# New ranks for GpSimd's free work in a top-k attention and channel-mix kernel

## The chip, the cores and the metric

The kernel runs on one core of one Trainium2 chip. The metric is the device time of one execution in microseconds. It has four engines that compute here: TensorE (PE in the profile, with PEld for its weight loads), VectorE (DVE), ScalarE (ACT) and GpSimd (POOL); SyncE (SP) issues the transfers.

## The reference

Two layers, one after the other, in float32. Attention with 8 batches, 8 heads, 576 positions and 64 numbers per head keeps, for each query, only the keys whose score reaches the 32nd largest; the channel mix shifts each sequence by one position, mixes it with itself in two ways and puts it through three matrices.

```python
scores = scale * np.matmul(q, k.transpose(0, 1, 3, 2))
kth = np.partition(scores, -32, axis=-1)[..., -32:-31]
scores = np.where(scores >= kth, scores, -1000000000.0)
attn = np.exp(scores - scores.max(-1, keepdims=True))
x = np.matmul(attn / (attn.sum(-1, keepdims=True) + 1e-09), v)   # then (8, 576, 512)
x_prev = np.concatenate([np.zeros((B, 1, D)), x[:, :-1, :]], axis=1)
xk = mu_k * x + (1.0 - mu_k) * x_prev
xr = mu_r * x + (1.0 - mu_r) * x_prev
k = np.maximum(xk @ w_k, 0.0)            # 512 -> 1024
v = k * k @ w_v                          # 1024 -> 512
r = 1.0 / (1.0 + np.exp(-(xr @ w_r)))
return r * v
```

## The kernel before

**Attention.** The 4608 rows of all batches are cut into 18 blocks of 256; a block has four groups (a pair of heads each), a group has four tiles of 128 rows by 576 keys, 288 tiles in all. A tile goes through a pipeline of some eight steps: scores on PE (`ps`), a copy by ScalarE (`sc`), the largest eight of each of seven pieces and three rounds over these on DVE (`cand`, `seen`), a signed copy on ScalarE and a product on GpSimd (`sg`, line 263) for the last eight of the 32, the exponentials (`se`), the masked product `E` on DVE, transposes on PE (`pt`) and their copy (`et`). At the end of a group come the inverses of the row sums: ScalarE adds the 1e-9 and DVE takes the reciprocal (`rs`, line 294), GpSimd spreads it (`rb`, line 298), PE transposes it (line 305), and after the value matmuls of the group (line 318) ScalarE copies the sums and GpSimd writes the product into `xT` (line 326).

**The mix.** A block is also a chunk (0 to 17) of the channel mix, which works in float32 split into a rounded part and a remainder, with three matmuls per product (`three`). A chunk has two halves of the 512 channels; a half is there when two of the four groups are placed in `xT`. `begin` queues the difference (`xd`), the share (`xm`) and the sum (`xm`) for a half, `finish` the rounded input (`xh`, ScalarE) and its remainder (`xl`, GpSimd). That is done twice for a chunk, first for the gates (`which` is 1), then for the hidden layer. `gates` is 8 pieces of PE work (`pz`), `hiddens` 16 pieces in four blocks of 256 hidden channels (`ph`); each block is followed by a relu and a rounded square on ScalarE (`r`, `hh`) and, on GpSimd, by the square (`r`, line 390) and its remainder (`hl`, line 391). `values` is twice 8 pieces (`pv`), one for each half of the rows: the first half is issued while the next chunk's gate inputs are made ready, the second after that chunk's gates, while its hidden inputs are made ready. If the next chunk isn't complete when the hidden blocks end, both halves are issued at once. The first value pieces use the first hidden blocks, the seventh the last.

**The order.** Everything is issued in an order that the program writes out itself. In one turn of its loop, here called slot n, every stage takes one step: scores of tile n, transposes of tile n - 5, and so on through the list ORDER; `mix` then issues pieces of the channel mix. Slot n's scores are the n-th group of line 213 or 217 in the trace. Free work waits in a queue for each lane (ScalarE, GpSimd) and has a price, a list of what it must follow, and a rank; a ledger says how much is issued in a slot:

```python
PACE, TENSOR, SHARE, PIECE, CAP, MOST = 4.60, 3.45, 0.74, 0.72, 4.45, 4
END, HASTE = 36, 0.56
...
while (item := self.first(self.queue.get(place, []))) and self.free[place] >= item.cost * SHARE * ...:
    self.do(item)
...
able = [item for item in queue if all(a.done for a in item.after)]
return min(able, key=lambda item: item.rank, default=None)
```

At the end of a slot a lane gets 4.60 us (never more than 4.45 in all), PE 3.45 (3.75). The fixed work is taken off as it is issued: on GpSimd 1.36 in each slot for `sg`, 0.34 in a slot with n divisible by 4 (`rb`), 0.6 two slots later (the product into `xT`); on ScalarE 2.56 in each slot, 0.25 in the slot after `rb`, 0.4 in the one after that, 0.46 for a relu, 0.48 for a gate's tanh. On PE 1.15 goes for scores and transposes, 1.54 more in the slot after `rb`, and 0.72 for a piece, from slot 252 on 0.56; no more than four pieces are issued in a slot. A piece that depends on free work (`past`) is issued only in a slot after the one in which that work was issued. Of items with equal rank the one queued first is taken.

Ranks before: `begin` 0, `finish` 0 (2 after slot 291, when DVE takes over GpSimd's free work), hidden blocks 1.

Of the kernel before, what the change touches and what calls it, by code (L numbers as in the profile page):

```python
# [9 lines left out]
F32 = mybir.dt.float32  # L10
# [3 lines left out]
AF = mybir.ActivationFunctionType  # L14
# [32 lines left out]
def topk_attention_channel_mix(ctx: ExitStack, tc: tile.TileContext, q, k, v, mu_k, mu_r, w_k, w_v, w_r, out):  # L47
    nc = tc.nc
# [279 lines left out]
    def begin(g, C, which, i, L):  # L328

        X, h0, n, pieces = Env(), 2 * i, C.n, C.pieces  # L330
        C.begun += 1
        parts, o = [], 0
        for xT, s, m in pieces:
            parts.append((o, xT, s, m))
            o += m

        def change():
            g.change[i] = g.one.tile([128, 2, CH], F32, name=f"xd{h0}")
            for o, xT, s, m in parts:
                g.by.tensor_sub(g.change[i][:, :, o:o + m], xT[:, h0:h0 + 2, s:s + m], xT[:, h0:h0 + 2, s + 1:s + 1 + m])  # L340

        def share():
            X.xm = g.two.tile([128, 2, CH], F32, name="xm")
            for h in (0, 1):
                g.by.tensor_scalar(X.xm[:, h, :n], g.change[i][:, h, :n], nmu[:, which, h0 + h:h0 + h + 1], 1.0, op0=OP.mult, op1=OP.mult)

        def add():
            for o, xT, s, m in parts:
                d = X.xm[:, :, o:o + m]
                g.by.tensor_add(d, d, xT[:, h0:h0 + 2, s + 1:s + 1 + m])  # L350

        l = g.shared[i]
        if which:
            l = [L.soft("pool", 0.0046 * n + 0.05 * len(pieces), change, *l)]
        g.shared[i] = [L.soft("pool", 0.0033 * n + 0.05, share, *l)]
        X.mixed = L.soft("pool", 0.0046 * n + 0.05 * len(pieces), add, *g.shared[i])
        g.reads[i] = X.mixed
        return X

    def finish(g, halves, n, L):  # L360
        xh = g.one.tile([128, HP, CH], F32R, name="xh")
        xl = g.one.tile([128, HP, CH], F32R, name="xl")
        for i, X in sorted(halves.items()):
            hi, lo = xh[:, 2 * i:2 * i + 2, :n], xl[:, 2 * i:2 * i + 2, :n]
            h = L.soft("act", 0.0017 * n + 0.07, lambda X=X, hi=hi: nc.scalar.activation(hi, X.xm[:, :, :n], AF.Copy), X.mixed, rank=2 * (g.by is nc.vector))  # L365
            last = L.soft("pool", 0.0046 * n, lambda X=X, hi=hi, lo=lo: g.by.tensor_sub(lo, X.xm[:, :, :n], hi.bitcast(F32)), h, rank=2 * (g.by is nc.vector))  # L366
        return xh, xl, last

    def three(ps, sh, sl, mh, ml, first, last):
        nc.tensor.matmul(ps, lhsT=sh, rhs=mh, start=first, stop=False)  # L370
        nc.tensor.matmul(ps, lhsT=sh, rhs=ml, start=False, stop=False)  # L371
        nc.tensor.matmul(ps, lhsT=sl, rhs=mh, start=False, stop=last)  # L372

    def hidden(g, f, part, xh, xl, hh, hl, n, X, L):
        if part == 0:
            X.ph = g.psM.tile([128, 2, CH], F32, name="ph", tag="pm")
        ph, e, half = X.ph, part // 2, part % 2
        w = slice((f + e) * 128, (f + e + 1) * 128)
        for h in range(half * HP // 2, (half + 1) * HP // 2):
            three(ph[:, e, :n], wk[0][:, h, w], wk[1][:, h, w], xh[:, h, :n], xl[:, h, :n], h == 0, h == HP - 1)  # L380
        if part < 3:
            return
        hi, lo = hh[:, f:f + 2, :n], hl[:, f:f + 2, :n]

        def relu():
            X.r = g.two.tile([128, 2, CH], F32, name="r")
            nc.scalar.activation(X.r[:, :, :n], ph[:, :, :n], AF.Relu)
        out_ = L.at(1, "evac", relu, "act", 0.46)
        h = L.soft("act", 0.5, lambda: nc.scalar.activation(hi, X.r[:, :, :n], AF.Square), out_, rank=1)
        q = L.soft("pool", 1.17, lambda: g.by.tensor_mul(X.r[:, :, :n], X.r[:, :, :n], X.r[:, :, :n]), h, rank=1)  # L390
        X.done = L.soft("pool", 1.17, lambda: g.by.tensor_sub(lo, X.r[:, :, :n], hi.bitcast(F32)), h, q, rank=1)  # L391

    def gate(g, t, m, h, xh, xl, G, L):
        if h == 0:
# [20 lines left out]
    def mix_steps(g, chunks, L):  # L415
# [22 lines left out]
        def poll():  # L438
            C = g.next
            if C:  # L440
                for i in range(2):
                    if i not in C.halves and C.have(i):
                        C.halves[i] = begin(g, C, 1, i, L)
                if len(C.halves) == 2:
                    g.next = None
# [14 lines left out]
        def hiddens(c, x):  # L460
            while not g.staged():
                yield 1
            c.hh = g.one.tile([128, NFB, CH], F32R, name="hh")
            c.hl = g.one.tile([128, NFB, CH], F32R, name="hl")
            c.written = {}
            for f in range(0, NFB, 2):
                X = Env()
                for part in range(4):
                    while len(g.ready) < (2 + f // 4) * HP:
                        yield 1  # L470
                    while part == 3 and len(g.hiddens) > 1 and not g.hiddens[-2].done:
                        yield 1
                    yield 0
                    hidden(g, f, part, *x, c.hh, c.hl, c.n, X, L)
                c.written[f // 2] = X.done
                g.hiddens.append(X.done)
# [5 lines left out]
        while c:  # L482
            while len(c.halves) < 2:
                for t in (0, 128):
                    yield from values(before, t)
                before = None
                yield 1
            halves = c.halves
            for which in (1, 0):
                *x, ready = finish(g, halves, c.n, L)  # L490
                yield from values(before, 0 if which else 128)
                while not L.past(ready):
                    yield 1
                if which:
                    halves = {i: begin(g, c, 0, i, L) for i in range(2)}
                else:
                    coming = open_chunk()
                yield from (gates if which else hiddens)(c, x)
            before, c = c, coming
# [388 lines left out]
    with ExitStack() as stack:  # L888
        g = Env()
# [6 lines left out]
    with tc.If(again > 0):  # L896
        with tc.For_i(0, B, 1) as b, ExitStack() as stack:
            g = Env()
            g.staged, g.by = (lambda: True), nc.gpsimd
            open_pools(stack, g, "_again")  # L900
            L = Direct()
# [70 lines left out]
```

## Time and profile before

| | |
|---|---|
| median of three runs | 1171.16 us (1170.75 to 1171.34) |
| profiled execution, its own time | 1172.81 us |
| span of that execution | 1171.0 us |
| PE, PEld busy | 1094.3 us (93%), 851.7 us (73%) |
| DVE, ACT, POOL busy | 1073.5 us (92%), 968.4 us (83%), 961.5 us (82%) |
| scores of tile 0 to 287 | until 1101.5 us |
| last value matmul | 1164.9 us |

The span is counted from the first to the last instruction of the profiled execution; the 1.8 us beside it are the start and end of the program. Busy shares are means over stages of different kinds: until about 120 us the weights are split into their two parts, from 1100 us on only the mix of the last two chunks is left. PE's busy time is modelled and overlaps, so that 97% of a stretch doesn't yet say that PE sets its length.

### The profile page before, as it was taken

Reading aid. Unit: us, or ns where it says so; the run is one execution under the profiler, and the core shown is the slowest. Engines: PE = TensorE matmul, PEld = TensorE weight load, DVE = VectorE, ACT = ScalarE, POOL = GpSimd, SP = SyncE. Lnnn points to the kernel's source line nnn. Section 1 sums busy time; section 2 is a strip of 40 time slices with the busy share of each in tenths; the row PEclk is TensorE's granted clock in tenths of the full one; section 3 lists DMA queues with packets and bytes.
Section 4 is the critical chain, followed back from the end, with each engine's and each line's share of the span. In section 5 each row is a group of like instructions: output and inputs, shape, how many; then the busy total and the mean of one; then the engine's idle time right before and its main releaser. Section 6 shows DMA issues by size and latency. Waiting matters only on the chain.

```text
span 1171.0 us, 32806 instructions
## 1 busy us (share of the span) xinstructions
PE 1094.3 (93%) x10753; PEld 851.7 (73%) x10753; DVE 1073.5 (92%) x5957; ACT 968.4 (83%) x1969; POOL 961.5 (82%) x1013
## 2 busy tenths in 40 slices
PE   5777898999999999999999999999999999999997
PEld 2444686868787878787878777878787778677876
DVE  6999999999999999999999999999999998888832
ACT  5898898889898888898989888989898888778731
POOL 4898897898889898989898989898989797689820
PEclk9889999999999999999999999999999999989999
DMA  6433223323332233222221223323332323211000
GB/s 177 137 110 111 53 70 96 80 62 84 82 85 67 67 89 84 54 58 56 67 60 53 55 75 88 78 69 80 79 89 66 82 71 80 78 40 31 29 20 22
DMA packets 168276, 85.87 MB, mean 73 GB/s; under 512 B 126112, under 2 KB 160928, under 8 KB 168096
## 3 DMA queue, kind: packets, MB, share of 16 engines
q1 hardware_dynamic: 168096, 83.67, 27.2%
q8 instruction: 88, 1.44, 0.5%
q14 instruction: 92, 0.75, 0.2%
HBM read 74.19 MB, written 9.44 MB: 71 GB/s over the span
## 4 chain that ended last, share of the span: by engine, by line
PE 42%; POOL 28%; DVE 19%; ACT 6%; issue 3%; SPq 1%; DMA 0%; ACTq 0%; POOLq 0%
POOL sg L263 9%; PE ps L318 8%; PE ps L213 6%; POOL hl L391 5%; DVE cand L246 4%; DVE E L274 4%; POOL r L390 3%; PE ph L370 3%; PE pv L370 3%; PE pt L284 3%; DVE seen L827 3%; POOL xl L366 3%; PE pv L372 3%; PE ph L371 3%; PE ph L372 3%
## 5 line engine op out<-in xcount | busy, mean ns | idle before, releaser
L246 DVE MAX8 cand<-sc 128x8 f32<-128x82 f32 (+1 forms) x2016 | 468.7, 233 | 18.3 <-ACT sc L222 18.1
L263 POOL TENSOR_TENSOR sg<-sc,sg 128x576 f32<-128x576 f32 x288 | 410.5, 1428 | 60.4 <-ACT sg L260 58.5
L222 ACT ACTIVATE sc<-ps 128x576 f32<-128x576 f32 x288 | 188.2, 653 | 140.5 <-PE ps L213 123.9
L274 DVE SCALAR_TENSOR_TENSOR E<-sc,seen,se 128x576 f32<-128x576 f32 x288 | 233.0, 809 | 1.7 <-DVE cand L246 0.9
L260 ACT ACTIVATE sg<-sc,seen 128x576 f32<-128x576 f32 x288 | 226.6, 787 | 2.5 <-DVE seen L827 2.3
L271 ACT ACTIVATE se<-sc,seen 128x576 f32<-128x576 f32 x288 | 217.0, 754 | 8.5 <-DVE E L274 7.7
L827 DVE MAX8 seen<-sg 128x8 f32<-128x576 f32 x288 | 216.7, 753 | 3.5 <-POOL sg L263 2.8
L213 PE MATMUL ps<-K,qs 64*128 64x288 f32 x1024 | 200.3, 467 | 15.8 <-ACT sc L222 10.6
L287 ACT ACTIVATE et<-pt 128x640 f32<-128x640 f32 x288 | 204.3, 709 | 5.0 <-PE pt L284 3.1
L284 PEld LDWEIGHTS pt<-ident,E 64*128 64x128 f32 x2880 | 133.9, 140 | 76.5 <-ACT sg L260 20.0
L249 DVE MAX8 seen<-cand 128x8 f32<-128x56 f32 x864 | 178.1, 206 | 0.1
L370 PE MATMUL ph<-xh,wk 128*128 128x256 f32 x576 | 171.5, 298 | 1.2 <-ACT xh L365 1.2
L318 PE MATMUL ps<-et,v_in 128*64 128x128 f32 (+1 forms) x2560 | 162.4, 272 | 4.0 <-ACT sc L222 3.9
L371 PE MATMUL ph<-xl,wk 128*128 128x256 f32 x576 | 161.0, 280 | 1.3 <-POOL xl L366 0.9
L372 PE MATMUL ph<-xh,wk 128*128 128x256 f32 x576 | 160.6, 279 | 0.0
L284 PE MATMUL pt<-ident,E 64*128 64x64 f32 x2880 | 140.6, 225 | 17.5 <-DVE E L274 10.5
L318 PEld LDWEIGHTS ps<-et,v_in 128*64 128x64 f32 x2560 | 136.0, 141 | 26.3 <-issue 16.0
L213 PEld LDWEIGHTS ps<-K,qs 64*128 64x128 f32 x1024 | 80.0, 190 | 83.7 <-issue 30.3
L372 PE MATMUL pv<-wv,hl 128*128 128x512 f32 x288 | 114.4, 397 | 14.2 <-POOL hl L391 14.2
L370 PE MATMUL pv<-wv,hh 128*128 128x512 f32 x288 | 125.1, 434 | 0.0
L252 DVE MATCH_REPLACE8 cand<-seen,cand 128x56 f32<-128x56 f32 x576 | 115.9, 201 | 0.0
L370 PEld LDWEIGHTS ph<-xh,wk 128*128 128x128 f32 x576 | 108.4, 188 | 8.9 <-ACT xh L365 1.6
(98 smaller groups left out, 2175.0 us busy)
## 6 DMA issues: line engine op xcount, KB each, us to landing
v_in<-in_v SPq DMA_DIRECT2D x192, 128.0 KB, 2.7
K<-in_k SPq DMA_DIRECT2D x112, 144.0 KB, 2.9
qs<-in_q SPq DMA_DIRECT2D x96, 128.0 KB, 2.9
out<-eb SPq DMA_DIRECT2D x36, 256.0 KB, 2.2
vr_in<-in_v SPq DMA_DIRECT2D x96, 32.0 KB, 2.4
hh<-in_moe_w_v SPq DMA_DIRECT2D x6, 512.0 KB, 4.2
qs<-in_q SPq DMA_DIRECT2D x32, 96.0 KB, 2.6
hh<-in_moe_w_k SPq DMA_DIRECT2D x5, 512.0 KB, 4.0
```

What stands on the lines that cost most here:

```text
L213: nc.tensor.matmul(g.ps[:, e], lhsT=P.qs[h, T.j, x:x + 128], rhs=Q.K[h, T.j], start=True, stop=True)
L246: nc.vector.max(T.cand[:, 8 * i:8 * i + 8], T.sc[:, CUTS[i]:CUTS[i + 1]])
L260: nc.scalar.activation(T.side, T.sc, AF.Sign, bias=T.top[:, 23:24], scale=-1.0, accum_out=T.cnt)
L263: nc.gpsimd.tensor_mul(T.side, T.sc, T.side)
L271: nc.scalar.activation(g.pe, T.sc, AF.Exp, bias=T.nb, scale=SCALE)
L274: nc.vector.scalar_tensor_tensor(T.e, T.sc, T.thr, g.pe, op0=OP.is_ge, op1=OP.mult, accum_out=T.rs)
L284: nc.tensor.transpose(g.pt[:, n, c * 64:(c + 1) * 64], T.e[h, k0:k0 + 128], ident[h, h])
L287: nc.scalar.activation(et.rearrange("p c (n q) -> p n c q", n=2), pt[:, :, :320].rearrange("p n (c q) -> p n c q", q=64), AF.Copy)
L318: nc.tensor.matmul(g.sums[hs[j], u, q], lhsT=lhsT, rhs=P.et[u, j][:, c, q], start=(c == 0), stop=(c == NKC))
L370: nc.tensor.matmul(ps, lhsT=sh, rhs=mh, start=first, stop=False)
L372: nc.tensor.matmul(ps, lhsT=sl, rhs=mh, start=False, stop=last)
L827: nc.vector.max(M.top[:, 24:32], M.side)
```

## The change

The ranks of the free work are set anew: hidden blocks' squares and remainders -1, rounded inputs and their remainders 0 as before, differences, shares and sums 1. Inside `finish` the remainder of the second half now also follows that of the first, and the caller is given the last of this chain. Nothing else is touched.

```diff
         l = g.shared[i]
         if which:
-            l = [L.soft("pool", 0.0046 * n + 0.05 * len(pieces), change, *l)]
-        g.shared[i] = [L.soft("pool", 0.0033 * n + 0.05, share, *l)]
-        X.mixed = L.soft("pool", 0.0046 * n + 0.05 * len(pieces), add, *g.shared[i])
+            l = [L.soft("pool", 0.0046 * n + 0.05 * len(pieces), change, *l, rank=1)]
+        g.shared[i] = [L.soft("pool", 0.0033 * n + 0.05, share, *l, rank=1)]
+        X.mixed = L.soft("pool", 0.0046 * n + 0.05 * len(pieces), add, *g.shared[i], rank=1)
...
+        last = ()
         for i, X in sorted(halves.items()):
             hi, lo = xh[:, 2 * i:2 * i + 2, :n], xl[:, 2 * i:2 * i + 2, :n]
             h = L.soft("act", 0.0017 * n + 0.07, lambda X=X, hi=hi: nc.scalar.activation(hi, X.xm[:, :, :n], AF.Copy), X.mixed, rank=2 * (g.by is nc.vector))
-            last = L.soft("pool", 0.0046 * n, lambda X=X, hi=hi, lo=lo: g.by.tensor_sub(lo, X.xm[:, :, :n], hi.bitcast(F32)), h, rank=2 * (g.by is nc.vector))
-        return xh, xl, last
+            last = (L.soft("pool", 0.0046 * n, lambda X=X, hi=hi, lo=lo: g.by.tensor_sub(lo, X.xm[:, :, :n], hi.bitcast(F32)), h, *last, rank=2 * (g.by is nc.vector)),)
+        return xh, xl, last[0]
...
-        h = L.soft("act", 0.5, lambda: nc.scalar.activation(hi, X.r[:, :, :n], AF.Square), out_, rank=1)
-        q = L.soft("pool", 1.17, lambda: g.by.tensor_mul(X.r[:, :, :n], X.r[:, :, :n], X.r[:, :, :n]), h, rank=1)
-        X.done = L.soft("pool", 1.17, lambda: g.by.tensor_sub(lo, X.r[:, :, :n], hi.bitcast(F32)), h, q, rank=1)
+        h = L.soft("act", 0.5, lambda: nc.scalar.activation(hi, X.r[:, :, :n], AF.Square), out_, rank=-1)
+        q = L.soft("pool", 1.17, lambda: g.by.tensor_mul(X.r[:, :, :n], X.r[:, :, :n], X.r[:, :, :n]), h, rank=-1)
+        X.done = L.soft("pool", 1.17, lambda: g.by.tensor_sub(lo, X.r[:, :, :n], hi.bitcast(F32)), h, q, rank=-1)
```

## Rows read from the trace of the kernel before

**Rows 1.** The page: busy us (share of the span) and instructions of each engine.

```profile
PE 1094.3 (93%) x10753; PEld 851.7 (73%) x10753; DVE 1073.5 (92%) x5957; ACT 968.4 (83%) x1969; POOL 961.5 (82%) x1013
```

**Rows 2.** Busy us per engine in the stretch 200 to 960 us, then granted clock.

```profile
200.00:960.00 760.00, 740.76 (x7601) 588.25 (x7600) 733.81 (x4218) 667.32 (x1370) 670.46 (x704) 1.00 0.28 73
```

**Rows 3.** Waits, 200 to 1000 us: who for whom, total us, times, longest.

```profile
PE pv L372 <- POOL hl L391: 14.2, 13, 1.3
DVE rs L294 <- ACT rs L291: 10.3, 14, 1.0
DVE eb L411 <- PE pv L372: 9.3, 12, 0.9
PEld pt L305 <- POOL rb L298: 4.6, 12, 0.6
```

**Rows 4.** PE's timeline in slots 139 to 141: start, us, what, idle before.

```profile
542.89 0.50 PE L372 MATMUL pv<-wv,hl 128*128 128x512 f32 x1 [1.05 <-POOL hl L391]
...
548.59 0.47 PE L284 MATMUL pt<-ident,E 64*128 64x64 f32 x10
549.05 0.34 PE L305 MATMUL pt<-ident,rb 64*128 64x64 f32 x4
```

**Rows 5.** GpSimd's timeline in slots 132 to 140.

```profile
516.90 0.41 POOL L298 TENSOR_SCALAR rb<-rs 128x256 f32<-128x256 f32 x1 [0.23 <-DVE cand L246]
517.60 1.04 POOL L390 TENSOR_TENSOR r<-r 128x512 f32<-128x512 f32 x1 [0.29 <-ACT hh L389]
...
529.43 1.08 POOL L350 TENSOR_TENSOR xm<-xm,xT 128x512 f32<-128x512 f32 x1
...
535.87 2.52 POOL L366 TENSOR_TENSOR xl<-xm,xh 128x512 fp32r<-128x512 f32 x2
...
541.56 1.27 POOL L391 TENSOR_TENSOR hl<-r,hh 128x512 fp32r<-128x512 f32 x1
...
548.60 0.40 POOL L298 TENSOR_SCALAR rb<-rs 128x256 f32<-128x256 f32 x1
```

**Rows 6.** Timeline of all engines: `rb` and PE behind it, first, last of 12; slot 253.

```profile
253.97 0.40 POOL L298 TENSOR_SCALAR rb<-rs 128x256 f32<-128x256 f32 x1
...
254.42 0.28 PE L305 MATMUL pt<-ident,rb 64*128 64x64 f32 x2
...
901.72 0.41 POOL L298 TENSOR_SCALAR rb<-rs 128x256 f32<-128x256 f32 x1
...
902.18 0.34 PE L305 MATMUL pt<-ident,rb 64*128 64x64 f32 x4
...
960.82 0.41 POOL L298 TENSOR_SCALAR rb<-rs 128x256 f32<-128x256 f32 x1
...
961.82 0.29 PE L305 MATMUL pt<-ident,rb 64*128 64x64 f32 x4
```

**Rows 7.** Timeline of all engines: the reciprocal in slot 144, `rb` in slot 148.

```profile
560.54 0.18 DVE L294 RECIPROCAL rs<-rs 128x4 f32<-128x4 f32 x1 [0.80 <-ACT rs L291]
...
575.29 0.41 POOL L298 TENSOR_SCALAR rb<-rs 128x256 f32<-128x256 f32 x1
```

**Rows 8.** PE's timeline, slot 58: scores, two of six value matmuls, next scores.

```profile
242.47 0.76 PE L213 MATMUL ps<-K,qs 64*128 64x288 f32 x4
...
243.81 0.40 PE L371 MATMUL pv<-wv,hh 128*128 128x512 f32 x1
244.05 0.40 PE L372 MATMUL pv<-wv,hl 128*128 128x512 f32 x1
...
245.07 0.76 PE L213 MATMUL ps<-K,qs 64*128 64x288 f32 x4
```

**Rows 9.** Busy us (PE, PEld, DVE, ACT, POOL), granted clock, DMA: three late stretches.

```profile
1016.00:1028.00 12.00, 8.83 (x68) 5.90 (x68) 11.22 (x63) 11.32 (x24) 7.88 (x8) 0.73 0.25 70
1036.00:1048.00 12.00, 10.03 (x96) 8.10 (x98) 10.59 (x62) 9.38 (x20) 9.16 (x11) 0.86 0.00 0
1068.00:1080.00 12.00, 9.65 (x97) 7.66 (x93) 10.27 (x61) 9.77 (x20) 12.00 (x12) 0.86 0.01 2
```

## The prediction

> **What bounds the kernel now.** I read the page first [rows 1]: PE and DVE are busy for over 90% of the span, GpSimd, whose work is re-ordered, for 82%. In the middle of the run [rows 2] PE is busy for 740.8 of 760 us and DVE for 733.8, so about 19 and 26 us are all that any change of order can win there. The list of waits of nearly the same stretch says what those gaps are [rows 3]: PE's is one wait that comes 13 times, value matmuls (`pv`) on `hl`, 14.2 us in all, 1.09 each; DVE's are the reciprocal waiting for ScalarE and `eb` waiting for `pv`. It is one wait in each chunk from the third to the fifteenth, and the new ranks move what it waits for.
>
> The two timelines of one chunk tell more [rows 4, 5]. GpSimd works from 516.90 to 549.00 with no gap but 0.29 us at its second operation: everything in these 32.1 us starts when the one before it ends. In that queue the last block's `hl` (541.56) stands behind two `xl` (535.87), and PE waits 1.05 us for it at 542.89. But at the end of the same queue stands `rb` (548.60, done 549.00), and PE's transposes of `rb` start at 549.05, 0.05 us later: PE waits there too, only briefly: its transposes before (548.59) leave some 0.15 us, and of these waits the list has 12 for PE's weight loads. Both waits hang on one queue, and the second one ends last. It is so in 12 of the 13 chunks, the start 0.05 to 0.15 us after `rb`; first and last are in [rows 6]. Behind that the loop closes: transposes at 549.05, scores and ScalarE's work until the reciprocal, which waits for it, at 560.54 (11.5 us), DVE's tiles until the next `rb` at 575.29 (14.75), which starts GpSimd's next stretch [rows 7]; 32.15 + 11.5 + 14.75 = 58.4 us. The twelve chunks of rows 6 are (902.18 - 254.42) / 11 = 58.9 us apart. The wait for `hl` isn't a link of this loop; it lies beside it.
>
> **The change part by part.** No instruction is added or removed; the ranks alone decide which free GpSimd operation is emitted when several are able. I follow the ledger of the slots (4.60 us of credit a slot, at most 4.45 kept, by the kernel's constants; `sg` takes 1.36, every fourth slot 0.34 for `rb`, the one after next 0.6; an operation is emitted while 0.74 of its price is left). For the chunk of rows 5 it gave, and the rows of the add and `xl` agree: slot 135 `xm` add and `r` (2), 136 `hl` (2), 137 both `xl`, 138 `r` (3) and `hl` (3), where (2) and (3) are the last two of the four hidden blocks. With the new ranks: 135 `r` and `hl` (2), 136 the add, 137 `r` and `hl` (3), 138 both `xl`. With the lead told of below, (3) moves on to 136, the add to 137, and the last `xl` stays in 138. The gates start in slot 139 in every case.
>
> *The wait for `hl`.* With `hl` (3) two operations earlier the 1.05 us at 542.89 go. What is late next is `rb`: the same operations stand ahead of it, 32.1 us of them, only in another order, so it still ends at 549.00, and PE, there about a microsecond earlier, waits about 1.2 us instead of 0.15. I take nothing for these 12 chunks. Bounds: below, all 14.2 us; above, in the chunks where the add takes 1.08 us (529.43 in [rows 5]) and `hl` 1.27, the `rb` of slot 136 comes 0.2 us later, 12 x 0.2 = 2.4 us; I take nothing there as well, since PE's microsecond of slack behind it covers it (without that cover, the 2.4). The 13th wait, at slot 251, has no `rb` close behind it: slots from 252 on hold four pieces of PE work; its `rb` ends at 961.23 and the transposes start at 961.82 [rows 6]: 0.6 us in hand, so I count 0.6 us won.
>
> The Trainium skill ("Perfetto Trace Analysis", "Identifying the Most-Contended Engine" and "Optimization Strategy") says to take the engine with the highest occupancy, find its gaps and make what they wait for come sooner. By that rule the gaps of PE would go and the time would fall by rows 3's 14.2 us; it is the first rival below, and rows 4 to 6, where PE waits again 6 us later, and for GpSimd, which has the lowest share of the four that compute, speak against it.
>
> *ScalarE's order.* The squares (`hh`) now go ahead of the rounded inputs (`xh`). Both take 0.64 us, and both have a consumer in the GpSimd queue above, which comes to them later than they are done; nothing.
>
> *The chain between the two `xl`.* They ran in this order already in the rows; nothing, and in odd row blocks it only keeps an early second half from passing the first.
>
> *The planner's lead.* In slot 58 PE got two value pieces instead of three [rows 8], because at that point `hl` (3) was not emitted before slot 58 and the seventh piece must wait a slot. With the new ranks `hl` (3) is emitted in slot 56, so slot 58 gets three, and the stream of PE pieces is one ahead. Every slot after it is full (three pieces, one in the slot with the sums: ten in four slots, forty a chunk), so the lead stays to the end. It costs nothing there and wins nothing, as the loop is not PE's.
>
> *The end.* From slot 252 on a piece costs the ledger 0.56 and four fit, so the stream catches up with its inputs and stops: before, in slots 267-268, 272 and 280-281 (rows 9 show the three gaps with what surrounds them). One piece ahead, the values before the first gap end in slot 265 and not 266, all that follows comes a slot earlier, and the hidden blocks of chunk 15 end in slot 276, not 278. There it turns: the inputs of chunk 16 are complete in slot 278 only. Before, they were just there, and half of the values of chunk 15 were kept to cover the rounding of the second mix. Now the values are all issued first (until slot 281), then comes a gap of two whole slots (282, 283), gates in 284 to 286, and, with nothing left to cover the second mix, one more gap in slot 287; the hidden blocks start in slot 288, not 287. Prices [rows 9], idle PE plus busy time lost to the lower of the two clock levels: first gap 12 - 8.83 = 3.2 idle and 8.83 x 0.27 = 2.4 slow, 5.6 us; second 2.0 and 1.4, 3.4; third 2.35 and 1.35, 3.7. The old third gap (3.7) gives way to one of the first kind (5.6): +1.9. The new fourth is of the second kind, 3.4, or at least its idle time, 2.0; I take 2.7, which is also what four more pieces after the last scores are worth (a value piece is three matmuls 0.24 us apart [rows 8], 0.7 us). Sum of the end: +4.6 us, between +2 and +5.3.
>
> Sum: 1172.81 (the profiled execution) - 0.6 + 4.6 = 1176.8, which is 4.0 above its own time; the median of the three runs lies 1.65 lower, so 1171.16 + 4.0 = 1175.2 us.
>
> **Rivals.** *PE is the bound after all* (it ends faster). Place: the transposes of `rb` in the slot two behind the gates' start. If GpSimd's stretch of 32.1 us gets shorter, or its start moves forward with PE, the microsecond is kept: 13 x 1.09 = 14.2 us, with or without the end's loss 1157 to 1162; with half of it 1164 to 1168. It decides from 0.3 us a chunk on (12 x 0.3 = 3.6, the end's loss). For it: PE is at 97% in rows 2 and its list has no other wait of size. Against it: the 0.05 us of rows 4 to 6. Chance 0.22.
>
> *The end goes as before.* The lead of one piece is not won in slot 58, or it is lost again, so that the order differs in the middle only: -0.6, 1170.6 us. For it: the lead hangs on one slot and on ScalarE's ledger in slot 56, where 0.42 is left of 4.45. Against: rows 8 show the two pieces. Chance 0.25; the same number follows if the order changes but every wait is merely renamed.
>
> *The middle loses too.* `sg` of slot 137 comes about 1.4 us later, since `r` and `hl` now stand ahead of it in 136 once the lead is there; DVE reads it, and `rb` is 0.2 later: 2.4 to 5 us on top of the end, 1178 to 1180. Chance 0.08.
>
> The forecast itself, 0.45.
>
> **How the numbers follow.** A difference under 0.2% (2.3 us) is about what a measurement of this kernel can't tell from none. Faster by more: the first rival, 0.22. Within: the second rival and the low end of my sum (+2 - 0.6), 0.25 + 0.05 = 0.30. Slower by more: the rest of the forecast and the third rival, 0.48. The range leaves out the far half of the first rival (0.13) and the far end of the third: 1163 to 1179; the likeliest case's own range is 1172.5 to 1178.
>
> **What would show it.** In the profile after: `r` and `hl` ahead of `xl` in each chunk; no `pv` waiting for `hl`, and in its place a wait of about 1.2 us for `rb` in the slot two behind; chunks 58.6 to 59 us apart as before; three value pieces in slot 58; near the end a gap of two slots after slot 281 and an empty slot 287. I am wrong if the chunks come closer than 58.3 us, if the wait for `rb` doesn't grow, or if the hidden blocks of chunk 16 start before the last scores.

## The result, and the profile after

The changed kernel takes 1176.9 us (median of seven runs, 1175.04 to 1178.88), the kernel before 1170.75 us in runs beside it: a ratio of 1.0059, with an interval from 1.0042 to 1.0076. The profiled execution took 1177.31 us, with a span of 1175.5. (From line 363 on, numbers in the changed kernel are one higher, so `hl` is made in line 392 and the three matmuls of a piece stand in lines 371 to 373.)

The engines' busy times and instruction counts on the page are almost those of [rows 1]: the work is the same, in a span 4.5 us longer.

```profile
PE 1089.7 (93%) x10753; PEld 850.1 (72%) x10753; DVE 1072.5 (91%) x5959; ACT 966.8 (82%) x1969; POOL 959.8 (82%) x1011
```

The list of waits from 200 to 1000 us (who for whom, total us, times, longest) answers to [rows 3]. PE's 13 waits for `hl` are gone. In their place stands the wait for `rb`, which is now the longest in the list for PE: 15.8 of its 21.1 us are the twelve waits of the chunks' transposes that the prediction named, and ten of the other eleven stand four slots before these. DVE, too, waits for GpSimd's `sg` in 35 places, and its wait of 9.3 us for `pv` is nearly gone.

```profile
PE pt L305 <- POOL rb L298: 21.1, 23, 1.5
DVE seen L828 <- POOL sg L263: 15.4, 35, 0.8
DVE rs L294 <- ACT rs L291: 9.6, 13, 0.9
...
DVE eb L412 <- PE pv L373: 1.2, 1, 1.2
```

GpSimd's timeline for the chunk of [rows 5] (start, us, what, idle before and its releaser) shows the new order: the last block's `hl` at 538.44, then the sum, then both `xl`. The queue is again without a gap from its second operation to `rb`, which is done at 552.85, 32.2 us after the stretch began; it was 32.1.

```profile
520.65 0.41 POOL L298 TENSOR_SCALAR rb<-rs 128x256 f32<-128x256 f32 x1 [1.19 <-DVE cand L246]
521.35 1.04 POOL L391 TENSOR_TENSOR r<-r 128x512 f32<-128x512 f32 x1 [0.30 <-ACT hh L390]
...
538.44 1.27 POOL L392 TENSOR_TENSOR hl<-r,hh 128x512 fp32r<-128x512 f32 x1
...
541.05 1.09 POOL L350 TENSOR_TENSOR xm<-xm,xT 128x512 f32<-128x512 f32 x1
...
544.19 2.53 POOL L367 TENSOR_TENSOR xl<-xm,xh 128x512 fp32r<-128x512 f32 x2
...
548.08 0.94 POOL L345 TENSOR_SCALAR xm<-xd,nmu 128x256 f32<-128x256 f32 x2
549.10 1.10 POOL L350 TENSOR_TENSOR xm<-xm,xT 128x512 f32<-128x512 f32 x1
550.17 0.94 POOL L345 TENSOR_SCALAR xm<-xd,nmu 128x256 f32<-128x256 f32 x2
551.07 1.41 POOL L263 TENSOR_TENSOR sg<-sc,sg 128x576 f32<-128x576 f32 x1
552.44 0.41 POOL L298 TENSOR_SCALAR rb<-rs 128x256 f32<-128x256 f32 x1
```

PE's timeline, from four places. Slot 58 holds three value pieces (the third begins at 244.86) where [rows 8] had two. Slots 61 and 125 are the ones to compare: each waits 1.5 us for `rb`, but slot 61 lasts 7.72 us, slot 125 6.13. In the chunk of [rows 4] the value matmul of slot 139 starts at 545.16 without a wait, and the transposes 7.75 us later wait 1.10. The last line answers to the last of the twelve in [rows 6].

```profile
242.38 0.76 PE L213 MATMUL ps<-K,qs 64*128 64x288 f32 x4
...
244.86 0.39 PE L371 MATMUL pv<-wv,hh 128*128 128x512 f32 x1
...
252.22 0.76 PE L213 MATMUL ps<-K,qs 64*128 64x288 f32 x4
...
254.86 0.34 PE L305 MATMUL pt<-ident,rb 64*128 64x64 f32 x4 [1.52 <-POOL rb L298]
...
256.39 1.98 PE L318 MATMUL ps<-et,v_in 128*64 128x128 f32 x16
...
259.94 0.76 PE L213 MATMUL ps<-K,qs 64*128 64x288 f32 x4
...
491.56 0.76 PE L213 MATMUL ps<-K,qs 64*128 64x288 f32 x4
...
494.19 0.34 PE L305 MATMUL pt<-ident,rb 64*128 64x64 f32 x4 [1.51 <-POOL rb L298]
...
495.35 1.09 PE L318 MATMUL ps<-et,v_in 128*64 128x128 f32 x16
...
497.69 0.76 PE L213 MATMUL ps<-K,qs 64*128 64x288 f32 x4
...
545.16 0.50 PE L371 MATMUL pv<-wv,hh 128*128 128x512 f32 x1
...
552.91 0.34 PE L305 MATMUL pt<-ident,rb 64*128 64x64 f32 x4 [1.10 <-POOL rb L298]
...
906.11 0.34 PE L305 MATMUL pt<-ident,rb 64*128 64x64 f32 x4 [1.39 <-POOL rb L298]
```

The stretches (PE, PEld, DVE, ACT, POOL busy; granted clock; DMA) say why. In slot 61 the clock fell to 0.50, the lower of its two levels, right behind the wait, and the sixteen matmuls of line 318 took 1.98 us in place of 1.09; in slot 125 it stayed at 1.00. The last four rows are the gaps of the end, which answer to [rows 9].

```profile
254.00:260.00 6.00, 5.14 (x49) 4.21 (x49) 5.72 (x30) 2.87 (x6) 4.92 (x6) 0.72 0.00 0
256.00:258.00 2.00, 2.00 (x18) 1.61 (x18) 2.00 (x16) 1.60 (x4) 2.00 (x3) 0.50 0.00 0
492.00:498.00 6.00, 4.49 (x63) 3.57 (x61) 5.73 (x37) 4.17 (x8) 6.00 (x7) 1.00 0.00 1
1020.00:1028.00 8.00, 5.79 (x48) 4.39 (x45) 7.37 (x42) 7.83 (x17) 5.30 (x5) 0.79 0.39 104
1037.00:1042.00 5.00, 2.80 (x32) 1.90 (x31) 4.37 (x24) 5.00 (x12) 3.46 (x4) 1.00 0.25 63
1083.00:1092.00 9.00, 6.58 (x50) 4.28 (x47) 8.38 (x50) 8.44 (x19) 5.90 (x5) 0.81 0.22 62
1101.00:1109.00 8.00, 5.21 (x42) 4.60 (x41) 7.03 (x39) 7.21 (x16) 6.25 (x6) 0.79 0.01 1
```

**Where the time went, by the two profiles.** The transposes of `rb` mark every fourth slot. To slot 61 the changed kernel is 0.4 us late (254.86 against 254.42). From there to slot 237 it takes 651.25 us in place of 647.76, 3.5 more; the clock fell twice in that stretch, behind slots 61 and 93, and by the granted clock each fall lost 1.7 us ((1 - 0.72) x 6). Without them the eleven chunks are as long as before, to 0.1 us. From slot 237 to slot 253 it wins 0.5, and from slot 253 to the last value matmul it loses 1.1 (204.18 against 203.06). With the 0.4 us ahead of slot 61 that makes 4.5 us, the difference of the spans.

### The profile page after: what moved, and what is told of

The parts are those of the page before. It is cut to its first block, busy times and chain, and to the rows that moved or that the text cites. A ratio compares the mean times of both kernels' runs of the same rounds, so it can differ in the third digit from the quotient of the medians.

```text
span 1175.5 us, 32787 instructions
## 1 busy us (share of the span) xinstructions
PE 1089.7 (93%) x10753; PEld 850.1 (72%) x10753; DVE 1072.5 (91%) x5959; ACT 966.8 (82%) x1969; POOL 959.8 (82%) x1011
## 4 chain that ended last, share of the span: by engine, by line
PE 43%; POOL 28%; DVE 19%; ACT 5%; issue 3%; DMA 1%; SPq 1%; POOLq 0%; ACTq 0%; DVEq 0%
POOL sg L263 10%; PE ps L318 9%; PE ps L213 6%; DVE cand L246 4%; DVE E L274 4%; PE pv L371 4%; POOL hl L392 3%; PE ph L371 3%; DVE seen L828 3%; POOL xl L367 3%; PE pv L372 3%; PE pv L373 3%; PE pt L284 3%; POOL r L391 3%; PE ph L372 3%
## 5 line engine op out<-in xcount | busy, mean ns | idle before, releaser
L287 ACT ACTIVATE et<-pt 128x640 f32<-128x640 f32 x288 | 205.2, 713 | 14.4 <-PE pt L305 11.0
L284 PEld LDWEIGHTS pt<-ident,E 64*128 64x128 f32 x2880 | 133.5, 139 | 77.1 <-ACT sg L260 16.9
L371 PE MATMUL pv<-wv,hh 128*128 128x512 f32 x288 | 124.8, 433 | 0.0
L372 PE MATMUL pv<-wv,hh 128*128 128x512 f32 x288 | 113.4, 394 | 0.0
```

The lines of the kernel that those rows point to most:

```text
L284: nc.tensor.transpose(g.pt[:, n, c * 64:(c + 1) * 64], T.e[h, k0:k0 + 128], ident[h, h])
L287: nc.scalar.activation(et.rearrange("p c (n q) -> p n c q", n=2), pt[:, :, :320].rearrange("p n (c q) -> p n c q", q=64), AF.Copy)
```

## The experiments

Ratios are to the kernel before, timed beside each run.

**Is GpSimd's queue up to `rb` the link that holds the loop?** The edit below, called the hold from here on, issues no free GpSimd work in slots 59, 75 and so on to 251, so that three free operations come to stand behind that `rb` and not ahead of it. The first run has it with the new ranks, the second with the old.

```diff
             for item in self.todo.pop((self.slot, place), []):
                 self.do(item)
+            if place == "pool" and 59 <= self.slot < 252 and self.slot % 16 == 11:
+                return
```

> The changed kernel, with one thing more: in each chunk of the middle no free GpSimd work is issued in the slot two before the transposes' wait (slots 59, 75, ... 251), so that the two shares and the sum of the hidden inputs, some 3.1 us, stand behind `rb` and not ahead of it. Theory (GpSimd's queue as far as that `rb` sets the pace, and the new ranks only moved PE's wait to it): `rb` starts up to 2.9 us earlier, right after the reciprocal; the 21.1 us of PE's waits for it shrink below 8, the chunks come 57 to 57.8 us apart in place of 58.9, the clock doesn't fall in the middle, 1153 to 1163 us. Rival (another engine or an earlier link holds the loop; the wait for `rb` is only what one sees of it): the wait moves on again, chunks 58.5 us or more, 1172 to 1178.

Measured: 1160.36 us, a ratio of 0.9917 to before (0.9896 to 0.9938). GpSimd's timeline shows `rb` at 538.58, after a gap of 0.16 us: it is held by DVE now and no longer by the queue.

```profile
535.60 2.81 POOL L263 TENSOR_TENSOR sg<-sc,sg 128x576 f32<-128x576 f32 x2
538.58 0.41 POOL L298 TENSOR_SCALAR rb<-rs 128x256 f32<-128x256 f32 x1 [0.16 <-DVE cand L246]
538.96 0.94 POOL L345 TENSOR_SCALAR xm<-xd,nmu 128x256 f32<-128x256 f32 x2
```

Its transposes in PE's timeline run without a wait (in slot 141 at 540.56, 1.6 us after `rb` is done), and slots 61 and 237 are (886.13 - 251.79) / 11 = 57.67 us a chunk apart.

```profile
251.79 0.31 PE L305 MATMUL pt<-ident,rb 64*128 64x64 f32 x4
...
540.56 0.29 PE L305 MATMUL pt<-ident,rb 64*128 64x64 f32 x4
...
886.13 0.29 PE L305 MATMUL pt<-ident,rb 64*128 64x64 f32 x4
```

In the waits from 200 to 1000 us, 5.1 us are left for `rb` (in the slot four earlier), and from 200 to 960 us PE is busy for 751.6 of 760 us, DVE for 744.2.

```profile
PE pt L305 <- POOL rb L298: 5.1, 10, 1.2
PE ps L318 <- ACT sc L222: 3.0, 7, 1.6
```

```profile
200.00:960.00 760.00, 751.62 (x7781) 600.07 (x7780) 744.19 (x4283) 680.35 (x1395) 684.04 (x718) 1.00 0.29 74
```

The theory holds, and the clock did not fall between 200 and 1000 us.

> The kernel before, with the same hold in slots 59, 75, ... 251 and nothing else. Theory (two waits of PE side by side on one queue, each of which holds the loop alone): the wait for `hl` in the slot of the first gates stays, 13 times about 1.1 us, and only the 0.05 to 0.15 us behind it go: 1167 to 1171 us, not more than 3 us faster than before. Rival (the hold alone is worth it, whatever the ranks): 1155 to 1162.

Measured: 1166.64 us, ratio 0.9975 (0.9965 to 0.9986): 0.4 us below the range of times expected, but 2.7 us below the 1169.35 of the kernel before beside it, so within the 3 us. The waits for `hl` stay, 14.4 us in 13; the transposes behind them wait no more in any of the 13 chunks. So each half alone is worth little or costs something (hold -0.25%, ranks +0.59%, in which the falls of the clock and the end told of below are counted), and both together win 0.83%: either wait holds the loop without the other.

**Does the second wait bind in the kernel before, too?** There it was seen as 0.05 us only. One more instruction ahead of these transposes asks for its slack:

```diff
                     spread(g, V.P)
+                    if 60 <= n < 252 and n % 16 == 12:
+                        nc.gpsimd.tensor_scalar(V.P.rb, V.P.rs[:, :, None].to_broadcast([128, 4, 64]), 1.0, 1.0, op0=OP.mult, op1=OP.mult)
```

> The kernel before, with one GpSimd instruction more in each chunk of the middle: the spread of the inverses (0.41 us) is done twice in slots 60, 76, ... 236, the ones in which GpSimd comes to it without a gap and PE's transposes wait 0.05 us behind it. Theory (this queue is a link of the loop in the kernel before too, beside the longer wait for `hl`): each of the 12 chunks gets 0.41 us longer, 4.9 us in all, 1172.5 to 1176, and the wait for `hl` stays at 13 to 15 us. Rival (the wait for `hl` alone holds the loop; `rb` merely ends at the same time): 1168 to 1171, the wait for `rb` grows and that for `hl` shrinks.

> The changed kernel with the hold of the first experiment, and the same 0.41 us more ahead of the same 12 transposes. Theory (behind the hold `rb` is done 1.1 to 2.2 us before its transposes, so this place is out of the loop): no change against the hold alone, 1158.5 to 1162. Rival (GpSimd's work as such sets the pace, wherever it stands): 4.9 us more, 1164 to 1167.

In the kernel before: 1177.21 us, ratio 1.0065 (1.0047 to 1.0082), 1.2 us above the range expected. In the profile slots 61 to 237 take 653.05 us against 647.76, 0.48 us a chunk, which is the time from the start of one spread to that of the next (0.49 below); the wait for `hl` stays at 14.3 us. Twelve times 0.48 are 5.8 of the 7.6 us between the medians; the rest stays open. With the hold: 1161.7 us, within the range expected; the ratio is 0.9933 (0.9915 to 0.9951) where the hold alone had 0.9917, which the intervals don't tell apart, and slots 61 to 237 take 634.24 us against 634.34. The two timelines of all engines show the place, first in the kernel before, then with the hold (L786 and L789 are the added spread):

```profile
548.66 0.41 POOL L298 TENSOR_SCALAR rb<-rs 128x256 f32<-128x256 f32 x1
549.15 0.41 POOL L786 TENSOR_SCALAR rb<-rs 128x256 f32<-128x256 f32 x1
...
549.62 0.34 PE L305 MATMUL pt<-ident,rb 64*128 64x64 f32 x4 [0.48 <-POOL rb L786]
```

```profile
536.45 0.41 POOL L789 TENSOR_SCALAR rb<-rs 128x256 f32<-128x256 f32 x1
...
537.96 0.29 PE L305 MATMUL pt<-ident,rb 64*128 64x64 f32 x4
```

The same 0.41 us costs the whole of itself where PE's transposes started 0.05 us behind `rb`, and nothing where some 1 us lies between (1.10 here, 0.6 to 1.4 in the twelve chunks).

**Which part of the change is it?** Ranks of -1 for lines 389 to 391 of the kernel before, and nothing else.

> The kernel before, with rank -1 for the squares and their remainders alone; differences, shares and sums stay at 0 and the two remainders of the inputs are not chained. The order is that of the changed kernel but for a sum that goes ahead of a remainder in some twenty slots. Theory (the squares' rank is the whole change): 1175 to 1178.5, waits for `rb` 19 to 22 us. Rival (the sums' lower rank matters, since a sum ahead of a remainder keeps the gates' inputs back): below 1173 or above 1180.

Measured: 1177.23 us, ratio 1.0061 (1.0046 to 1.0076), waits for `rb` 18.2 us, a little under the 19 expected at least. The squares' rank is the whole change; the rank of the shares and the chain move nothing that the time shows.

**What does the lead of one piece cost?** It is given up once where it arises and once where it begins to matter.

```diff
-                work(MOST)
+                work(2 if n == 58 else MOST)
...
-                work(MOST)
+                work(3 if n == 252 else MOST)
```

> The changed kernel, with only two pieces of the channel mix allowed in slot 58, so that PE's stream is not one piece ahead and the last slots follow nearly the order of the kernel before; this takes out the lead alone. By the prediction (the lead costs 4.6 us at the end and nothing in the middle): 1171.5 to 1173. Theory from the profile after (the lead costs about 0.7 us in slot 58 and 1 us at the end, and the other 3.5 us are falls of the clock behind the longer wait for `rb` in the middle): 1174 to 1177, the wait for `rb` at 20 us as in the changed kernel, one to three stretches at the lower clock in the middle.

> The changed kernel with only three pieces in slot 252 and nothing else: the middle is the changed kernel's, the end nearly that of the kernel before. By the prediction (4.6 us at the end): 1171.5 to 1173.5. Theory by the ten profiles (about 3 us): 1172.5 to 1175. Rival (the end costs nothing, all of the loss is in the middle): 1176 to 1178.

Dropped in slot 58: 1176.72 us, ratio 1.005 (1.0032 to 1.0068), not in the range that the prediction's price gave but in that of the profile after. Dropped in slot 252: 1173.23 us, ratio 1.0014 (1.0002 to 1.0026), in the ranges of both prices and outside the rival's. In the second the middle is the changed kernel's, so giving up the lead wins the difference of the ratios, 1.0059 - 1.0014, some 5 us (3.7 by the medians). The run without the lead from slot 58 on has a longer middle in its profile, by 2.9 us (slots 57 to 253: 729.22 us against 726.37), with three falls of the clock for two. Why it has another microsecond there stays open.

Neither run goes back to the end of the kernel before. In both PE is busy for 11.47 of 12 us around slots 280 and 281, where the third gap of [rows 9] left 9.65 at a clock of 0.86; the stretch of the run dropped in slot 252 is the first line below. There the hidden blocks of chunk 16 begin in slot 286, ahead of the last scores (1100.41 and 1101.91), and in the kernel before they began in slot 287. So the 3.7 to 5 us are the difference to a new end that lacks that gap.

```profile
1071.00:1083.00 12.00, 11.47 (x119) 8.63 (x118) 10.54 (x59) 10.68 (x24) 11.76 (x12) 1.00 0.10 24
```

```profile
1100.41 0.28 PE L371 MATMUL ph<-xh,wk 128*128 128x256 f32 x1
...
1101.91 0.76 PE L213 MATMUL ps<-K,qs 64*128 64x288 f32 x4
```

The profiles of all thirteen kernels of this document allow both comparisons, from the transposes of slot 253 to the last value matmul. The seven with the lead have 204.2 to 207.5 us, 205.8 in the mean. The three with the old ranks have 201.2 to 203.1, 201.9 in the mean, and the three with the new ranks and without the lead 202.9 to 204.1, 203.5 in the mean; why these are not below the old ones, with a gap closed, stays open. Against the old end, which is what the prediction priced, the end with the lead costs 3.9 us.

**Do the falls of the clock explain the middle?**

> The changed kernel with the hold in two chunks alone, slots 59 and 91, behind which the clock fell in the profile after (at 255 and 374 us). Theory (each of these falls costs 1.7 us beside the wait of 1.5 us that comes before it): both waits and both falls go, 2 x 3.2 us, 1169 to 1172.5, no stretch at the lower clock between 240 and 950 us. Rival (the falls come some chunks later instead, or cost nothing since another link waits anyway): 1173 to 1176.

> The changed kernel with the hold in two other chunks, slots 139 and 155, where PE waits 1.1 and 1.3 us and the clock doesn't fall; the counterpart to the hold in slots 59 and 91. Theory (a wait and a fall of the clock are two prices): only the two waits go, 2.4 to 3 us, 1173 to 1175.5, and the clock still falls behind slots 61 and 93. Rival (the hold in slots 59 and 91 won by the waits alone): the same as that run, 1170.5 to 1172.5.

Measured: 1172.06 us, ratio 1.0021 (1.0006 to 1.0036), and 1172.98 us, ratio 1.0022 (1.0008 to 1.0035). The two don't differ, so the second expectation failed: its time lies at the border of its two ranges. The first time is in its range, but not for the reason given. The profiles tell why: with the hold in slots 59 and 91 the clock fell at 839 us instead, behind another of the long waits; with the hold in 139 and 155 it fell behind slot 93 (371 us), but not behind slot 61, although that waits 1.49 us. These two runs alone can't tell the theories apart.

The thirteen profiles together can. From 240 to 960 us PE has 23 waits of 1.45 us or more in them. The clock fell behind 13 of these and behind no shorter wait. The kernel before has no wait that long there (1.32 us is its longest) and no fall. Twelve of the 13 falls came behind a wait for `rb`; one came behind a wait for `hl`, in the kernel before with the doubled spread (the first line below; the clock fell at 245.3 us).

```profile
245.02 0.60 PE L372 MATMUL pv<-wv,hl 128*128 128x512 f32 x1 [1.45 <-POOL hl L391]
```

What the falls cost is shown by slots 61 and 125 above, and by the length of slots 61 to 237 in the four profiles that have the new order in all chunks: 651.25 and 651.56 us with two falls, 652.52 and 654.01 with three, against 647.76 in the kernel before, without one. That is 1.6 to 2.1 us for each, and nearly all that the middle lost. Behind which of the long waits a fall comes is not settled by the program's order. In the changed kernel the clock stayed at 1.00 in slot 125; in the run dropped in slot 252, with the same order there and a wait of 1.50 us, it fell:

```profile
490.00:496.00 6.00, 4.50 (x43) 3.55 (x43) 5.74 (x35) 4.01 (x8) 6.00 (x7) 0.72 0.00 1
```

**What is left behind the hold?** One run has the hold and gives the share of the gates' inputs to ScalarE, which takes the next 0.94 us out of GpSimd's queue; the other has the hold and takes the lead out of the end. The edit of the first:

```diff
+        act = which and 48 <= getattr(L, 'slot', 0) < 252
...
+                if act:
+                    nc.scalar.activation(X.xm[:, h, :n], g.change[i][:, h, :n], AF.Copy, scale=nmu[:, which, h0 + h:h0 + h + 1])
...
+        g.shared[i] = [L.soft("act", 0.8, share, *l, rank=1) if act else L.soft("pool", 0.0033 * n + 0.05, share, *l, rank=1)]
```

> The changed kernel with the hold, and the share of the gates' inputs in the middle done by ScalarE (two activations with a scale per partition) in place of GpSimd (0.94 us), which takes 0.94 us out of the queue ahead of the `rb` four slots earlier (slots 136, 152, ...), where PE now waits 0.5 to 0.8 us. Theory (the link that is left is that `rb`, for the same reason): those waits go, 0.4 to 0.6 us for each of 12 chunks, 1153 to 1157. Rival (DVE, busy 98% of the stretch behind the hold, or ScalarE's order holds the loop by now): 1159 to 1163.

Measured: 1162.3 us, ratio 0.9942 (0.9923 to 0.996), in the rival's range and not faster than the hold alone (0.9917; the intervals overlap). The waits for that `rb` are gone as expected, but PE waits 14.6 us for ScalarE's `sc` where it waited 3.0, and the chunks of the profile are 58.0 us apart where the hold alone had 57.67. That fits the rival's ScalarE.

```profile
PE ps L318 <- ACT sc L222: 14.6, 15, 1.6
...
DVE found L268 <- ACT se L271: 10.0, 28, 1.0
```

> The changed kernel with the hold, and only three pieces in slot 252, so that the lead of one piece is given up there: the middle is that of the first experiment, the last slots are nearly those of the kernel before. Theory (what the lead costs at the end is real: from the transposes of slot 253 to the last value matmul six profiles with the lead have 204.2 to 207.5 us, four without it 201.2 to 204.1): 2 to 4 us faster than the hold alone, 1155.5 to 1159. Rival (nothing is to be had there, as the run without the lead from slot 58 on came out at the changed kernel's time): 1159.5 to 1162.

Measured: 1152.83 us, ratio 0.9848 (0.983 to 0.9866), a larger gain than expected. The spans of the two profiles differ by 4.6 us (1157.1 and 1152.5), the medians by 7.5; the rest stays open. This version, the new ranks with the hold and without the lead at the end, beats the kernel before by 1.5% and the changed one by 2.1% (0.9848 / 1.0059).

## Why the prediction was right, and where it was wrong

**The wait for `hl`** went, and the one for `rb` took its place, as forecast: the twelve transposes wait 0.99 to 1.52 us, 1.32 in the mean, where 1.2 was said. Nothing was won by it: the chunks are 58.9 us long without the falls of the clock. The hold shows that this was the reason, and the doubled spread that the 0.05 us of [rows 4, 6] were the sign of it. One row was read wrongly: of the 12 waits of PE's weight loads for `rb` in [rows 3] only five (0.24 to 0.29 us each) stand ahead of these transposes, the other seven ahead of those four slots before. That the start follows `rb` by 0.05 to 0.15 us holds in all 12 chunks.

**The first rival** (PE is the bound after all) named its own condition, a shorter GpSimd stretch; the hold fulfils it and wins 16.5 us against the changed kernel (1176.9 to 1160.36). In the profiles slots 61 to 237 get 16.9 us shorter (634.34 against 651.25); 3.4 of it are the two falls of the clock, and 13.5 are the chunks, 1.2 us each. The gaps of PE were worth their length only once both were closed. The Trainium skill ("Perfetto Trace Analysis", "Optimization Strategy") says to find the engine's gaps and let what they wait for come sooner. The run with both waits closed agrees (ratio 0.9917); the one with the first alone, 1.0059, shows that the rule has to be applied to all that one queue holds back. The prediction took the engine by its occupancy. For TensorE the Trainium skill ("Perfetto Trace Analysis", "Identifying the Most-Contended Engine") doesn't take the matmuls' busy share as a good measure and looks, beside another figure, at that of the weight loads. That is 73% here [rows 1], below DVE's 92%.

**Slot 251** was forecast with 0.6 us to win: 0.5 in the profile.

**The planner's lead** came as worked out: three pieces in slot 58, gaps in slots 266 and 267, 271, 282 and 283, and none issued in slot 287. Of its price, +4.6 us, the changed kernel's own profile shows 1.1; by the means of the profiles with the lead and of those with the old ranks it is 3.9. The size was about right, though a single pair of traces doesn't show it. The step counted the clock's loss as a fixed part of each gap (5.6, 3.4 and 3.7 us), and it isn't: the clock stayed at 1.00 in the stretch from 1037 to 1042, which [rows 9] had at 0.86, and the first gap lost 1.7 us to it where that of before lost 3.4 (0.31 x 11, from the row below, of the kernel before).

```profile
1018.00:1029.00 11.00, 7.83 (x60) 5.01 (x58) 11.00 (x64) 10.75 (x23) 8.43 (x9) 0.69 0.18 56
```

**The step that failed** is "I take nothing for these 12 chunks". It moved a wait of a microsecond from one place to another and asked only whether the loop gets longer. Where the wait came to 1.5 us in one piece ahead of the sums, the clock fell behind it twice in the profile: 3.4 us, in a term that the prediction put at nothing. The chunks came out 651.25 / 11 = 59.2 us apart, where 58.6 to 59 had been named as a sign. In the profiled execution the end lost 1.1 us in place of 4.6, which nearly made up for it; that the spans differ by 4.5 us, close to the sum of +4.0, is luck. The medians are 6.1 us apart. Two falls, the end by the means of the profiles and slot 251 give 3.4 + 3.9 - 0.5 = 6.8 us, an estimate that has the failed term in it and agrees with them better.

**The other rivals.** "The end goes as before" is refuted by the order of the gaps. Of "the middle loses too" the named mechanism is visible (DVE waits for `sg` 15.4 us where it waited 1.4), but costs nothing in the length of the chunks.

## What to carry to other kernels

Where two waits hang on one in-order queue, look at what the engine does just after the wait that you mean to remove: a second start 0.05 us behind its releaser, with the queue still gapless ahead of it, can be a link of the loop, as it was here, and doubling a short instruction there shows whether it is. Then move work behind the last of these waits, as well as ahead of the first. And a wait that only moves is not free on TensorE: gathered into one longer piece, here up to 1.5 us where it had been 1.3 at most, it can cost the clock as well.

## What the hardware did that was not expected

Behind waits of 1.5 us PE's granted clock fell to the lower of its levels (0.50, 1.2 GHz) in slots 61 and 93 and not in slot 125 with the same wait and the same instructions; slot 61 took 7.72 us and slot 125 6.13, 1.6 us for the fall. Over all profiles 13 of 23 such waits brought one. The Trainium skill ("TensorE: Matmul & The Clock Gate", "Part 1: The HAM clock gate (the "warmup" mystery)") says that the throttled clock is the default and that activity releases it; the fall behind an idle stretch agrees with it. That the same wait does and doesn't bring it may be a part of why runs of one kernel differ by up to 4 us here (1175.04 to 1178.88). The clocks of the seven runs lean that way: the two longest, 1178.58 and 1178.88 us, have the lowest means, 0.974 and 0.976, and the shortest the highest, 0.983. But the one in the profile has 0.982 and took 1177.31, so this is not shown.
